# Fourier mixing and a gated FFN in one kernel: batch 0 turned on TensorE, DFT-47 of two batches inside the first tile

## The chip, the cores and the metric

The kernel runs on one core of a Trainium2 chip. The metric is the device time of one execution in microseconds; of the kernel before, three runs gave a median of 2671.09 us (2669.9 to 2671.72).

## The reference

`x` is 8 batches of 3008 positions by 256 channels, float32. The output is computed in two parts:

```
X  = rfft(x, axis=1)
Yr = Xr @ w_r - Xi @ w_i + b_r
Yi = Xr @ w_i + Xi @ w_r + b_i
Y  = soft threshold of Yr and Yi at 0.01
t  = irfft(Y, n=3008)            # 24064 tokens of 256
h  = t @ w_in                    # 256 x 2048
out = (h * sigmoid(1.702 h)) @ w_out
```

The weights of the second part come as float64 and are handed to the kernel as 64-bit words.

## The kernel before

**The Fourier part.** 3008 is 47 times 64, so the transform is done in two steps. Per batch: a DFT-47 (`stage_a`, constant `ka`) over 16 column blocks; a DFT-64 for 24 values of the 47 side, two per step `sp`, so 12 steps (`stage_b`, helper `dft64`, L278-286); the mixing with `w_r` and `w_i`, bias and threshold (`stage_mix`, `mixed` and `threshold`); and an inverse DFT-64 (`stage_inv`). The last inverse step, an inverse DFT-47, is done where tokens are fetched (`tokens`, constant `kz`). The DFT-47 contracts the position `n2` and the DFT-64 the position `n1`. Between the two the data change place between partitions and columns: `stage_a` writes its rows to a DRAM buffer `s1` (L308) and the next step reads them back in another view (L324, `rows`). All inverse results go to a DRAM buffer `s2`, from which `load_u` (L492) reads the columns for the tokens, all 96 rows at a time; so no token of a batch starts before that batch's last inverse step.

**Two forms of it.** `spectral_plain` (batches 0 and 1) works in float32 matrix products, of which the trace records two passes each. `spectral` (batches 2 to 7) splits each operand in a rounded high part and a rest and makes three products in the F32R type (`mm3`).

**The FFN.** Tokens come in 47 tiles of 512, and each tile takes 8 steps `q` over 256 of the 2048 hidden columns. `up(q)` makes 12 products of 512 columns, applies the activation on ScalarE (tile `gb`), and forms sums and high and low parts on ScalarE and VectorE (`hb`, `lb`, `gt`, `ht`, `lt`). `down` of the step before makes 21 products of 256 columns. Its 16 weight blocks (block 2q is `w_in` of step q, block 2q+1 `w_out`) are loaded by GpSimd's DMA queue and converted from float64 by ScalarE and VectorE (`from_float64`, `up_weights`, `down_weights`; tiles `aem` and `w`).

**The order of work.** The code is written in one order, and a scheduler with a model of time moves instructions forward on each engine where their inputs allow; each engine then runs its list in order. Before the first tile stand all of batch 0, the DFT-47 of batch 1 (`a1`) and weight blocks 0 to 7; the rest of batch 1 and blocks 8 to 15 are in a list `front`, taken during the first four FFN steps. The steps of batches 2 to 7 follow in a queue between FFN steps. Nothing holds the weight blocks in place, and the scheduler put all sixteen ahead of the first tile. The DMAs of loads, `s1`, `s2` and output all go through SP's queue, in its order.

Of the kernel before, what the change touches and what calls it, by code (L numbers as in the profile page):

```python
# [48 lines left out]
def constants():  # L49
# [59 lines left out]
    pack[:96, 524:618] = ai  # L109
    plain = np.zeros((128, 96), np.float32)  # L110
    plain[:96] = a
    return np.concatenate([plain, pack, packs], 1), b.astype(np.float32)


@with_exitstack
def fourier_mix_then_gated_ffn(ctx: ExitStack, tc: tile.TileContext, x, w_r, w_i, b_r, b_i, w_in, w_out, pack, kbs, out):
    nc = tc.nc
    NB = x.shape[0]
    NT = out.shape[0]
    a96, pack, packs = pack[:96, 0:96], pack[:, 96:96 + PK], pack[:, 96 + PK:96 + PK + PKR]  # L120
# [34 lines left out]
    def const(shape, dt, name):  # L155
        return cst.tile(shape, dt, name=name, tag=name.rstrip("_"))

    ka = const([96, 192], F32, "ka")
    ki = const([128, 512], F32, "ki")
    kz = const([96, 94], F32, "kz")  # L160
    fg = const([128, NS], F32, "fg")
# [128 lines left out]
                s2.rearrange("(s r) p j d -> s (r p j) d", r=2))  # L290


    def spectral_plain(b, s2):

        s1 = dr.tile([48, 2, NJ, D], F32, name="s1")
        s1w, s1r, s2w = dram_views(s1, s2)
        xs, ks, raw, rows, cos, mv = {}, {}, {}, {}, {}, {}

        def load_x(n):
            xs[n] = su.tile([96, 2, 512], F32, name="xp", tag="xp", bufs=6)  # L300
            nc.sync.dma_start(xs[n].rearrange("p a n -> p (a n)"), x[b, :, 1024 * n:1024 * (n + 1)])

        def stage_a(q):
            ps = bank()
            mm(ps[:96], ka[:, 0:96], xs[q // 2][:, q % 2])
            ev = buf2("aev")[:96]
            nc.scalar.copy(ev.rearrange("p j d -> p (j d)"), ps[:96])
            nc.sync.dma_start(s1w[:, 512 * q:512 * (q + 1)], ev.rearrange("p j d -> p (j d)"))  # L308

        def load_k(sp):  # L310
            ks[sp] = buf([128, 2, 2 * N1], F32, "kr") if b else su.tile([128, 2, 2 * N1], F32, name="k0", tag="k0", bufs=8)
            nc.sync.dma_start(ks[sp], kbs[sp])

        def load_b(sp):
            if sp not in ks:
                load_k(sp)
            k = ks[sp]
            if b:
                t = buf2("br")
                nc.sync.dma_start(t, s1r[2 * sp:2 * sp + 2].rearrange("s p d -> p s d"))  # L320
            else:
                if sp % 2 == 0:
                    rows[sp // 2] = su.tile([128, 4, D], F32, name="rows", tag="rows", bufs=6)
                    nc.sync.dma_start(rows[sp // 2], s1r[2 * sp:2 * sp + 4].rearrange("s p d -> p s d"))  # L324
                t = rows[sp // 2][:, 2 * (sp % 2):2 * (sp % 2) + 2]
            raw[sp] = t, k

        def stage_b(sp):
            for n in range(sp, sp + (2 if b else 3)):
                if n < 12 and n not in raw:  # L330
                    load_b(n)
            cos[sp] = dft64(*raw[sp])

        def stage_mix(sp):
            co = cos.pop(sp)
            pa, pb = bank(), bank()
            for v, ps in ((2, pa[:, 0:D]), (1, pb[:, 0:D]), (0, pb[:, D:])):
                for c in range(2):
                    mm(ps, co[:, c, v], wf[:, v, c], start=c == 0, stop=c == 1)
            v = mixed(pa, pb)  # L340
            threshold(v)
            mv[sp] = v

        def stage_inv(m):


            if b:
                po = [bank()[:, 0:D].rearrange("p (h d) -> p h d", h=1) for _ in range(2)]
            else:
                po = [ps_o.tile([128, 2, D], F32, name="pi", tag=f"po{2 * (m % 2) + i}") for i in range(2)]  # L350
            G = 1 if b else 2
            for h in range(G):
                sp = G * m + h
                v = mv.pop(sp)
                if sp:
                    kt = buf([128, 128], F32, "kt", bufs=1)
                    nc.scalar.mul(kt, kv[:, 1], fg[:, sp:sp + 1])
# [7 lines left out]
            if b:  # L365
                ev = buf2("iev")
                for i in range(2):
                    nc.scalar.copy(ev[:, i], po[i][:, 0])
                nc.sync.dma_start(s2w[2 * m:2 * m + 2].rearrange("s p d -> p s d"), ev)
                return  # L370
# [5 lines left out]
        return load_x, stage_a, load_k, load_b, stage_b, stage_mix, stage_inv  # L376


    def spectral(b, s2):
        s1 = dr.tile([48, 2, NJ, D], F32, name="s1")  # L380
        s1w, s1r, s2w = dram_views(s1, s2)
# [137 lines left out]
    class Ffn:  # L519
# [5 lines left out]
        def up(self, q):  # L525
            gb = fbuf([128, 4, HT], F32, "gb")
            for i in range(2):
                f = 2 * q + i
                ps = bank()
                fs = slice(128 * f, 128 * f + 128)  # L530
                for c in range(2):
                    mm3(ps, wi_h[:, c, fs], wi_l[:, c, fs], self.th[:, c], self.tl[:, c], start=c == 0, stop=c == 1)
                o = gb[:, 1:3] if i else gb[:, 0:4:3]
                nc.scalar.activation(o, ps.rearrange("p (h n) -> p h n", h=2), AF.Gelu_apprx_sigmoid)  # L534
# [11 lines left out]
            split(ht, lt, gt)  # L546
            self.g[q] = [(hb[:, i], lb[:, i]) for i in range(3)] + [(ht[:, i], lt[:, i]) for i in range(4)]

        def down(self, q):
# [36 lines left out]
            done += 1  # L586
        load_u(done)

    lx0, a0, lk0, lb0, b0, m0, i0 = spectral_plain(0, new_s2(0))
    lx1, a1, lk1, lb1, b1, m1, i1 = spectral_plain(1, new_s2(1))  # L590

    nc.sync.dma_start(ka[:, 0:96], a96)
    for n in range(6):
        lx0(n)
    load_weights(0)
    load_weights(1)
    mixer_in()
    for q in range(16):
        a0(q)
        if q in (1, 3):  # L600
            lx0(6 + q // 2)
        if q in (5, 7, 9):
            lx1((q - 5) // 2)
        if 5 <= q < 13:
            lk0(q - 5)
        if q in (6, 11):
            weights(q // 6 - (q > 6))
    for sp in range(0, 8, 2):
        lb0(sp)
    constants_in()  # L610
    for q in range(6):
        a1(q)
    for n in range(14):
        if n < 12:
            b0(n)
        if 1 <= n < 13:
            m0(n - 1)
        if n % 2 and n >= 3:
            i0((n - 3) // 2)
        if n % 2 == 0 and n < 12:  # L620
            weights(2 + n // 2)
        if 3 <= n < 8:
            lx1(n)
    for q in range(6, 16):
        a1(q)
    held.close()
    ff = ctx.enter_context(tc.tile_pool(name="ff", bufs=2, reuse_waits="tile"))

    front = []
    for n in range(14):  # L630
        if n < 12:
            front.append((b1, n))
        if 1 <= n < 13:
            front.append((m1, n - 1))
        if n >= 2:
            front.append((i1, n - 2))
        if n % 3 == 0 and n < 12:
            front.append((weights, 8 + 2 * n // 3))
            front.append((weights, 9 + 2 * n // 3))
    nf = len(front)  # L640

    tokens_to(TOK)
    queue, nextb, behind = [], 2, None
    for n in range(NT * NQ):
        k, q = divmod(n, NQ)
        if q == 0:
            cur = Ffn(k)
        cur.up(q)
        while front and len(front) * 4 > nf * (3 - n):
            step, m = front.pop(0)  # L650
            step(m)
        if not front and not queue and nextb < NB:
            if nextb == 2:
                rounded_parts()
# [52 lines left out]
```

## Time and profile before

| | |
|---|---|
| median of three runs | 2671.09 us |
| profiled execution | 2669.87 us |
| its span | 2668.1 us |
| TensorE busy | 2607.2 us (98%) |
| VectorE busy | 2001.8 us (75%) |
| ScalarE busy | 1563.2 us (59%) |
| mean granted TensorE clock | 0.988 |

The sums below are made against the profiled execution: 2669.87 us, of which 1.8 us lie outside its span. The matmul records are pipelined: the ends that the trace shows include the drain of the last one, so the pace of a stream is read from one start to the next.

### The profile page before, as it was taken

The numbers are of one execution on the slowest core, as the hardware profiler recorded it, in microseconds if no ns is written. First come the engines' busy times: TensorE is split into PE (matmuls) and PEld (weight loads), VectorE is DVE, ScalarE is ACT, GpSimd is POOL, SyncE is SP. The second block draws the span as 40 slices with busy tenths as digits, with TensorE's granted clock in tenths as the row PEclk, the third lists the DMA queues.
The fourth block names the chain that finished last, engine by engine and source line by source line (L and its number), as shares of the span: only waits on it lengthen the run. The fifth ranks groups of instructions, "written<-read, shape, count | busy, mean of one in ns | idle before, by whom it ended". The sixth has DMA issues, their size and how long they took to land. (4 is left out here: it accounts for less than half of the span.)

```text
span 2668.1 us, 42434 instructions
## 1 busy us (share of the span) xinstructions
PE 2607.2 (98%) x16562; PEld 2332.4 (87%) x16562; DVE 2001.8 (75%) x3287; ACT 1563.2 (59%) x2431; POOL 61.5 (2%) x69
## 2 busy tenths in 40 slices
PE   5889999999999999999999999999999999999998
PEld 2667899999989999899989999899998899999997
DVE  5945777777777777777877777778877787777776
ACT  3334655555575566656576555755567556655554
POOL 1000000000000000000000000000000000000000
PEclk7989999999999999999999999999999999999999
DMA  9343212121232223322232222422324122200000
GB/s 312 105 125 104 81 46 61 42 79 46 66 122 61 79 71 95 116 65 73 81 112 84 69 72 81 131 66 66 94 73 124 56 77 87 78 21 32 18 20 16
DMA packets 165176, 214.03 MB, mean 80 GB/s; under 512 B 16112, under 2 KB 115184, under 8 KB 164976
## 3 DMA queue, kind: packets, MB, share of 16 engines
q1 hardware_dynamic: 162512, 202.41, 25.2%
q0 software_dynamic: 2464, 8.91, 1.1%
q8 instruction: 130, 2.13, 0.3%
q14 instruction: 70, 0.57, 0.1%
HBM read 117.42 MB, written 93.85 MB: 79 GB/s over the span
## 5 line engine op out<-in xcount | busy, mean ns | idle before, releaser
L534 ACT ACTIVATE gb<-pa 128x512 f32<-128x512 f32 x752 | 448.1, 598 | 507.4 <-PE pa L145 505.3
L142 DVE TENSOR_TENSOR lt<-gt,ht 128x1024 fp32r<-128x1024 f32 x376 | 465.5, 1238 | 259.5 <-ACT ht L141 257.5
L145 PE MATMUL pa<-th,wi_h 128*128 128x512 f32 x1504 | 593.6, 395 | 0.5 <-ACT th L141 0.5
L145 PE MATMUL pa<-tl,wi_h 128*128 128x512 f32 x1504 | 592.1, 394 | 0.0
L145 PE MATMUL pa<-th,wi_l 128*128 128x512 f32 x1504 | 589.0, 392 | 0.0
L141 ACT CAST ht<-gt 128x1024 fp32r<-128x1024 f32 x376 | 394.1, 1048 | 254.2 <-DVE gt L545 253.7
L145 PE MATMUL po<-lt,wo_h 128*128 128x256 f32 x1504 | 411.1, 285 | 0.6 <-DVE lt L142 0.6
L145 PE MATMUL po<-ht,wo_l 128*128 128x256 f32 x1504 | 406.0, 283 | 0.0
L543 DVE TENSOR_TENSOR gt<-gb 128x512 f32<-128x512 f32 x376 | 259.2, 689 | 164.6 <-ACT gb L534 156.7
L142 DVE TENSOR_TENSOR lb<-gb,hb 128x768 fp32r<-128x768 f32 x376 | 362.0, 963 | 26.0 <-ACT hb L141 24.7
L145 PE MATMUL po<-ht,wo_h 128*128 128x256 f32 x1504 | 362.2, 284 | 1.6 <-ACT ht L141 1.4
L145 PEld LDWEIGHTS pa<-th,wi_l 128*128 128x128 f32 x1504 | 283.9, 189 | 55.5
L141 ACT CAST hb<-gb 128x768 fp32r<-128x768 f32 x376 | 314.4, 836 | 26.3 <-PE po L145 19.1
L145 PEld LDWEIGHTS pa<-th,wi_h 128*128 128x128 f32 x1504 | 284.8, 189 | 45.1 <-ACT th L141 0.7
L145 PEld LDWEIGHTS pa<-tl,wi_h 128*128 128x128 f32 x1504 | 285.0, 189 | 41.1
L145 PE MATMUL po<-lb,wo_h 128*128 128x256 f32 x1128 | 316.4, 284 | 1.8 <-DVE lb L142 1.8
L145 PE MATMUL po<-hb,wo_l 128*128 128x256 f32 x1128 | 315.7, 283 | 0.0
L145 PE MATMUL po<-hb,wo_h 128*128 128x256 f32 x1128 | 313.9, 291 | 0.0
L145 PEld LDWEIGHTS po<-lt,wo_h 128*128 128x128 f32 x1504 | 286.4, 190 | 9.2 <-DVE lt L142 0.8
L145 PEld LDWEIGHTS po<-ht,wo_l 128*128 128x128 f32 x1504 | 286.1, 191 | 5.7
L145 PEld LDWEIGHTS po<-ht,wo_h 128*128 128x128 f32 x1504 | 264.5, 190 | 12.0 <-ACT ht L141 1.6
L145 PEld LDWEIGHTS po<-hb,wo_h 128*128 128x128 f32 x1128 | 212.2, 190 | 12.4 <-issue 1.0
(93 smaller groups left out, 3531.5 us busy)
## 6 DMA issues: line engine op xcount, KB each, us to landing
s<-aev SPq DMA_DIRECT2D x128, 192.0 KB, 2.2
s<-iev SPq DMA_DIRECT2D x96, 256.0 KB, 2.2
ur<-s SPq DMA_DIRECT2D x128, 192.0 KB, 2.9
out<-o SPq DMA_DIRECT2D x94, 256.0 KB, 2.2
br<-s SPq DMA_DIRECT2D x84, 256.0 KB, 3.0
xr<-in_x SPq DMA_DIRECT2D x96, 192.0 KB, 3.0
yd<-mv SPq DMA_DIRECT2D x144, 128.0 KB, 2.4
yr<-yd SPq DMA_DIRECT2D x72, 256.0 KB, 3.0
```

Source lines behind the costliest of these rows:

```text
L141: nc.scalar.copy(hi, src)
L142: return nc.vector.tensor_tensor(lo, src, hi.bitcast(F32), ALU.subtract)
L145: nc.tensor.matmul(ps, lhsT=w, rhs=t, start=start, stop=stop)
L534: nc.scalar.activation(o, ps.rearrange("p (h n) -> p h n", h=2), AF.Gelu_apprx_sigmoid)
L543: nc.vector.tensor_tensor(gt[:, 0:2], b12, gb[:, 0:3:2], ALU.subtract)
```

## The change

Batch 0 gets a function of its own, `first_batch`. Its DFT-47 is written with the data as the stationary side: 64 products of 96 columns, whose results lie with channels on partitions. ScalarE copies them to an SBUF tile `z` (L310), and `turn` (L321) transposes 128x128 pieces of `z` on TensorE against an identity `one` into PSUM, from where ScalarE copies them to `rows` (L323). No DRAM buffer `s1` is used for batch 0. Only six of the sixteen DFT-47 blocks of batch 1 stay ahead of the first tile; its other ten and all sixteen of batch 2 (`dft47`, plain float32) are spread over the first seven FFN steps. The rest of batch 1 is done by `spectral`, in the split form, from the second tile on. `issue_after` ties hold weight blocks 0 to 7 behind named steps of batch 0 and blocks 8 to 15 behind the activation and the last split of the FFN steps of the first tile.

```diff
-    def spectral_plain(b, s2):
-
-        s1 = dr.tile([48, 2, NJ, D], F32, name="s1")
...
+    def first_batch(s2):
...
+        def stage_a(n):
+            t = xs.pop(n)
+            for c in range(2):
+                ps = bank()[:, 0:384].rearrange("p (j f) -> p j f", j=4)
+                for j in range(4):
+                    mm(ps[:, j], t[:, j, 128 * c:128 * c + 128], ka)
+                done_at["z", n] = nc.scalar.copy(z[:, c, :, 4 * n:4 * n + 4], ps.rearrange("p j f -> p f j")).ins
...
+        def turn(sp):
+            pt = ps_o.tile([128, 2, D], F32, name="pt", tag=f"po{2 + sp % 2}")
+            for i in range(2):
+                f = 4 * (2 * sp + i)
+                for c in range(2):
+                    nc.tensor.transpose(pt[:, i, 128 * c:128 * c + 128], z[:, c, f:f + 4].rearrange("p f j -> p (f j)"), one)
+            rows[sp] = su.tile([128, 2, D], F32, name="rows", tag="rows", bufs=4)
+            done_at["r", sp] = nc.scalar.copy(rows[sp], pt).ins
...
+    def dft47(b, q, t):
+
+        ps = bank()
+        mm(ps[:96], ka, t.rearrange("p j d -> p (j d)"))
+        ev = buf2("aev")[:96]
+        nc.scalar.copy(ev.rearrange("p j d -> p (j d)"), ps[:96])
+        s1w = s1s[b].rearrange("c p j d -> (c p) (j d)")
+        done_at["e"] = nc.sync.dma_start(s1w[:, 512 * q:512 * (q + 1)], ev.rearrange("p j d -> p (j d)")).ins
...
-        for n in range(16):
-            add(0, split_x, n, 16)
-            add(650, stage_a, n, 16)
-        steps.append((4000, lambda: None))
+        if not begun:
+            for n in range(16):
+                add(0, split_x, n, 16)
+                add(650, stage_a, n, 16)
+            steps.append((4000, lambda: None))
...
+    with after(("z", 7)):
+        weights(2)
...
+        if n % 2 == 0 and 2 <= n < 12:
+            with after(("v", n - 2), ("r", n)):
+                weights(2 + n // 2)
...
-    for q in range(6, 16):
-        a1(q)
+    for q in range(6):
+        dft47(1, q, x1[q // 2][:, 2 * (q % 2):2 * (q % 2) + 2])
...
+    early = [(1, q) for q in range(6, 16)] + [(2, q) for q in range(16)]
...
+        if n < NQ:
+            for m in range(8 + n + (n > 0), min(10 + n, 2 * NQ)):
+                with after("g", "l"):
+                    weights(m)
+            while nearly < len(early) * (n + 1) // 7 and nearly < len(early):
+                do_early(nearly)
+                nearly += 1
+        elif not queue and nextb < NB:
+            if nextb == 1:
+                with after("e"):
+                    rounded_parts()
             queue = spectral(nextb, new_s2(nextb))
```

Three places in the lists of instructions show what moves. The first is the start of TensorE's list; `pa<-xp,ka` is the DFT-47 of before, `pa<-ka,xp` that of the change, `pt` the transposes, `k` and `rows` the DFT-64, `wf` the mixing. Before:

```order
L145 MATMUL pa<-xp,ka 96x512 x22
L145 MATMUL pa<-k_144,rows 128x2x64 x4
L145 MATMUL pa<-k_151,rows 128x2x64 x4
L145 MATMUL pa<-wf,co 128x256 x6
L145 MATMUL pa<-k_178,rows 128x2x64 x4
```

Changed:

```order
L145 MATMUL pa<-ka,xp 128x96 x64
L321 MATMUL pt<-one,z 128x128 x8
L145 MATMUL pa<-k_179,rows 128x2x64 x4
L321 MATMUL pt<-one,z 128x128 x4
L145 MATMUL pa<-k_181,rows 128x2x64 x4
L321 MATMUL pt<-one,z 128x128 x8
L145 MATMUL pa<-wf,co 128x256 x6
L145 MATMUL pa<-k_183,rows 128x2x64 x4
L321 MATMUL pt<-one,z 128x128
```

Twenty-two DFT-47 blocks (16 of batch 0, 6 of batch 1) become 64 small products, and five steps' transposes stand ahead of the first mixing.

The second is VectorE's list where the first tokens (`tl`) come; `aem` and `w` are a weight block, `wo_l` its end, `mv` the threshold of a mixing step. Before, the last of the sixteen blocks ends right ahead of them:

```order
L269 SCALAR_TENSOR_TENSOR mv<-mv,mt 128x512
L253 TENSOR_TENSOR w_1501<-aem 128x2x128
L253 TENSOR_TENSOR w_1501<-aem 128x256
L256 TENSOR_TENSOR w_1501<-w_1501 128x128
L255 TENSOR_TENSOR w_1501<-w_1501 128x128
L257 TENSOR_TENSOR w_1501<-w_1501 128x128
L258 TENSOR_TENSOR w_1501<-w_1501 128x128
L142 TENSOR_TENSOR wo_l<-w_1501,wo_h 128x896
L142 TENSOR_TENSOR tl<-pa,th 128x2x188 x2
L142 TENSOR_TENSOR tl<-pa,th 128x2x136
L142 TENSOR_TENSOR tl<-pa,th 128x2x52
L285 TENSOR_TENSOR co<-co 128x2x128
L543 TENSOR_TENSOR gt<-gb 128x512
```

Changed, where `wo_l<-w_744` ends block 7:

```order
L142 TENSOR_TENSOR wo_l<-w_744,wo_h 128x896
L269 SCALAR_TENSOR_TENSOR mv<-mv,mt 128x512
L274 TENSOR_TENSOR mv<-pa,bias 128x512
L275 TENSOR_TENSOR mv<-pa,mv 128x512
L268 TENSOR_SCALAR mt<-mv 128x512
L269 SCALAR_TENSOR_TENSOR mv<-mv,mt 128x512
L142 TENSOR_TENSOR tl<-pa,th 128x2x188 x2
L142 TENSOR_TENSOR tl<-pa,th 128x2x136
L142 TENSOR_TENSOR tl<-pa,th 128x2x52
L556 TENSOR_TENSOR gt<-gb 128x512
L557 TENSOR_TENSOR gt<-gb,gt 128x256
L558 TENSOR_TENSOR gt<-gt,gb 128x256
L142 TENSOR_TENSOR lb<-gb,hb 128x768
L142 TENSOR_TENSOR lt<-gt,ht 128x1024
L231 TENSOR_SCALAR aem<-wraw 128x512 x2
L142 TENSOR_TENSOR tl<-pa,th 128x2x188
L232 SCALAR_TENSOR_TENSOR aem<-wraw,aem 128x512
```

Eight blocks stand ahead of the tokens where sixteen did, and blocks 8 and 9 begin behind the first step's `lt`.

The third is SP's queue between the last writes of batch 0 (`s_82<-iev`) and the reads for the first tokens (`ur`); `aev` are DFT-47 results on their way to `s1`. Before:

```order
L374 DMA s_82<-iev 128x2x256 x10
L184 DMA pk<-in_pack 128x822
L374 DMA s_82<-iev 128x2x256 x2
L308 DMA s_85<-aev 96x512 x9
L492 DMA ur<-s_82 96x512
L308 DMA s_85<-aev 96x512
L492 DMA ur<-s_82 96x512 x3
```

Changed:

```order
L359 DMA s_82<-iev 128x2x256 x8
L386 DMA s_86<-aev 96x512 x5
L655 DMA xr<-in_x 96x512 x2
L386 DMA s_86<-aev 96x512
L655 DMA xr<-in_x 96x512
L505 DMA ur<-s_82 96x512 x4
L655 DMA xr<-in_x 96x512 x2
```

Nine writes of DFT-47 results stood between the two; now six stand there, with three loads for the next DFT-47 blocks (`xr`).

## Rows read from the trace of the kernel before

**Rows 1.** The page's 40 slices: TensorE's granted clock in tenths.
```profile
PEclk7989999999999999999999999999999999999999
```

**Rows 2.** Windows: length; busy of PE, PEld, DVE, ACT, POOL; clock, DMA share, GB/s.
```profile
57.80:135.00 77.20, 67.74 (x344) 50.92 (x344) 72.45 (x152) 28.25 (x51) 5.93 (x8) 0.93 0.42 138
...
135.00:148.60 13.60, 7.23 (x14) 2.37 (x13) 1.70 (x4) 7.68 (x15) 0.00 (x0) 0.87 0.67 208
148.60:246.90 98.30, 90.93 (x508) 75.67 (x508) 52.26 (x90) 35.88 (x75) 0.00 (x0) 0.94 0.32 98
148.60:160.70 12.10, 10.79 (x43) 9.52 (x44) 2.23 (x5) 4.04 (x7) 0.00 (x0) 0.58 0.36 115
246.90:252.70 5.80, 5.68 (x13) 3.80 (x14) 3.48 (x6) 3.36 (x7) 0.00 (x0) 0.51 0.53 159
252.70:2658.30 2405.60, 2403.57 (x15631) 2189.22 (x15629) 1840.03 (x2971) 1465.31 (x2248) 47.30 (x46) 1.00 0.24 71
```

**Rows 3.** DMA, 0 to 60 us: totals; issues, KB each, us to landing.
```profile
DMA packets 9295, 18.38 MB, mean 306 GB/s; under 512 B 1369, under 2 KB 4490, under 8 KB 9293
...
xp<-in_x SPq DMA_DIRECT2D x16, 384.0 KB, 6.5
```

**Rows 4.** Timeline, PE, start-up: start, us, what, x records, [idle <-releaser].
```profile
5.95 7.51 PE L145 MATMUL pa<-xp,ka 96*96 96x512 f32 x12 [5.95 <-DMA xp<-in_x]
...
57.91 3.72 PE L145 MATMUL pa<-k,rows 128*128 128x128 f32 x16 [8.98 <-ACT aem L230]
```

**Rows 5.** Windows, instructions on tile aem (weight blocks) alone, on VectorE.
```profile
57.80:138.00 80.20, 36.44 (x68) 0.93 0.41 133
sum 138.00, DVE 59.47; mean DVE 29.74
```

**Rows 6.** The same for tile w (the down blocks' seven sums).
```profile
57.80:138.00 80.20, 15.55 (x37) 5.63 (x6) 0.93 0.41 133
sum 138.00, DVE 23.04 ACT 7.50; mean DVE 11.52 ACT 3.75
```

**Rows 7.** Timeline, PE, inside batch 0's loop.
```profile
82.23 1.05 PE L145 MATMUL pa<-k,rows 128*128 128x128 f32 x8
83.22 0.70 PE L145 MATMUL pi<-mv,ki 64*128 64x256 f32 x4
...
84.28 2.86 PE L145 MATMUL pa<-wf,co 128*128 128x256 f32 x12
86.98 1.05 PE L145 MATMUL pa<-k,rows 128*128 128x128 f32 x8
```

**Rows 8.** Timeline, PE, in the steady part; the last row is plain F32.
```profile
1004.10 0.85 PE L145 MATMUL pa<-yh,ki__1623 128*128 128x512 f32 x3
1004.79 0.28 PE L145 MATMUL po<-hb,wo_h 128*128 128x256 f32 x1
...
1010.96 0.28 PE L145 MATMUL pa<-wf_h,zz 128*128 128x256 f32 x1
...
1013.10 0.28 PE L145 MATMUL po<-hb,wo_h 128*128 128x256 f32 x1
...
122.98 1.10 PE L145 MATMUL pa<-xp,ka 96*96 96x512 f32 x2
```

**Rows 9.** Timeline, PE and SP, from batch 0's last inverse to the first tokens.
```profile
134.54 0.60 PE L145 MATMUL pi<-mv,kt 64*128 64x256 f32 x4
...
138.13 7.20 SPq L308 DMA_DIRECT2D s<-aev  x9
...
145.43 0.36 SPq L492 DMA_DIRECT2D ur<-s  x1
...
148.62 1.10 PE L145 MATMUL pa<-kz,ur 96*128 96x94 f32 x8 [3.37 <-DMA ur<-s]
```

**Rows 10.** Windows, instructions on tile gt alone (seventeen FFN steps), 300 to 400 us.
```profile
300.00:400.00 100.00, 46.71 (x67) 17.77 (x17) 1.00 0.17 52
```

**Rows 11.** The page's fifth part: VectorE's lb, whole run.
```profile
L142 DVE TENSOR_TENSOR lb<-gb,hb 128x768 fp32r<-128x768 f32 x376 | 362.0, 963 | 26.0 <-ACT hb L141 24.7
```

More of the change, by code (lines that the diff above doesn't have):

```diff
@@ L111, in constants @@
     plain[:96] = a
-    return np.concatenate([plain, pack, packs], 1), b.astype(np.float32)
+    return np.concatenate([plain, np.eye(128, dtype=np.float32), pack, packs], 1), b.astype(np.float32)
 @with_exitstack
@@ L290, in dram_views @@
                 s2.rearrange("(s r) p j d -> s (r p j) d", r=2))
-    def spectral_plain(b, s2):
-        s1 = dr.tile([48, 2, NJ, D], F32, name="s1")
-        s1w, s1r, s2w = dram_views(s1, s2)
-        xs, ks, raw, rows, cos, mv = {}, {}, {}, {}, {}, {}
-        def load_x(n):
[L300 to L308, printed above, removed]
+    def first_batch(s2):
+        s2w = s2.rearrange("(s r) p j d -> s (r p j) d", r=2)
+        xs, ks, rows, cos, mv = {}, {}, {}, {}, {}
+        z = su.tile([128, 2, 96, NJ], F32, name="z")
+        one = su.tile([128, 128], F32, name="one")
+        nc.gpsimd.dma_start(one, eye)
+        def load_x(n):
+            xs[n] = xpair(0, n)
+        def stage_a(n):
[5 more added lines that the diff above has]
+                done_at["z", n] = nc.scalar.copy(z[:, c, :, 4 * n:4 * n + 4], ps.rearrange("p j f -> p f j")).ins
@@ L310, in load_k @@
         def load_k(sp):
-            ks[sp] = buf([128, 2, 2 * N1], F32, "kr") if b else su.tile([128, 2, 2 * N1], F32, name="k0", tag="k0", bufs=8)
+            ks[sp] = su.tile([128, 2, 2 * N1], F32, name="k0", tag="k0", bufs=3)
             nc.sync.dma_start(ks[sp], kbs[sp])
[L314 to L326, printed above, removed]
+        def turn(sp):
[6 more added lines that the diff above has]
+            done_at["r", sp] = nc.scalar.copy(rows[sp], pt).ins
@@ L328, in stage_b @@
         def stage_b(sp):
[L329 to L332, printed above, removed]
+            cos[sp] = dft64(rows.pop(sp), ks.pop(sp))
         def stage_mix(sp):
@@ L340, in stage_mix @@
             v = mixed(pa, pb)
-            threshold(v)
+            done_at["v", sp] = threshold(v).ins
             mv[sp] = v
         def stage_inv(m):
[L347 to L353, printed above, removed]
+            po = [ps_o.tile([128, 2, D], F32, name="pi", tag=f"po{i}") for i in range(2)]
+            for h in range(2):
+                sp = 2 * m + h
                 v = mv.pop(sp)
@@ L374, in stage_inv, with xpair, after, new_s1 @@
                 nc.sync.dma_start(s2w[4 * m + i:4 * m + 4:2].rearrange("s p d -> p s d"), ev)
-        return load_x, stage_a, load_k, load_b, stage_b, stage_mix, stage_inv
+        return load_x, stage_a, load_k, turn, stage_b, stage_mix, stage_inv
+    def xpair(b, n):
+        t = su.tile([96, 4, D], F32, name="xp", tag="xp", bufs=5)
+        nc.sync.dma_start(t.rearrange("p j d -> p (j d)"), x[b, :, 1024 * n:1024 * (n + 1)])
+        return t
+    s1s, done_at = {}, {}
+    def after(*keys):
+        held = ExitStack()
+        for k in keys:
+            held.enter_context(tc.issue_after(done_at[k]))
+        return held
+    def new_s1(b):
+        s1s[b] = dr.tile([48, 2, NJ, D], F32, name="s1")
+    def dft47(b, q, t):
[5 more added lines that the diff above has]
+        done_at["e"] = nc.sync.dma_start(s1w[:, 512 * q:512 * (q + 1)], ev.rearrange("p j d -> p (j d)")).ins
     def spectral(b, s2):
-        s1 = dr.tile([48, 2, NJ, D], F32, name="s1")
-        s1w, s1r, s2w = dram_views(s1, s2)
+        begun = b in s1s
+        if not begun:
+            new_s1(b)
+        s1w, s1r, s2w = dram_views(s1s[b], s2)
         ka, ki, fg, wf_h, wf_l = (parts[n] for n in "aifhl")
@@ L545, in up @@
             nc.vector.tensor_tensor(gt[:, 3], gt[:, 2], gb[:, 1], ALU.subtract)
-            split(ht, lt, gt)
+            done_at["l"] = split(ht, lt, gt).ins
             self.g[q] = [(hb[:, i], lb[:, i]) for i in range(3)] + [(ht[:, i], lt[:, i]) for i in range(4)]
@@ L587, in tokens_to @@
         load_u(done)
[L589 to L593, printed above, removed]
+    lx0, a0, lk0, t0, b0, m0, i0 = first_batch(new_s2(0))
+    new_s1(1)
+    new_s1(2)
+    nc.sync.dma_start(ka, a96)
+    for n in range(5):
         lx0(n)
@@ L596, in fourier_mix_then_gated_ffn @@
     load_weights(1)
[L597 to L611, printed above, removed]
-        a1(q)
-    for n in range(14):
+    for n in range(8):
+        a0(n)
+        if n < 3:
+            lx0(n + 5)
+        if n == 3:
+            mixer_in()
+            constants_in()
+            for k in range(3):
+                lk0(k)
+        if n in (2, 4):
+            with after(("z", n)):
+                weights(n // 4)
+    with after(("z", 7)):
+        weights(2)
+    x1 = {}
+    for n in range(15):
+        if n == 0:
+            t0(0)
+        if n < 11:
+            t0(n + 1)
         if n < 12:
             b0(n)
+        if n < 9:
+            lk0(n + 3)
         if 1 <= n < 13:
@@ L619, in fourier_mix_then_gated_ffn, with load_early, do_early @@
             i0((n - 3) // 2)
[L620 to L623, printed above, removed]
-    for q in range(6, 16):
-        a1(q)
+        if n % 2 == 0 and 2 <= n < 12:
+            with after(("v", n - 2), ("r", n)):
+                weights(2 + n // 2)
+        if n in (4, 6, 8):
+            x1[n // 2 - 2] = xpair(1, n // 2 - 2)
+    for q in range(6):
+        dft47(1, q, x1[q // 2][:, 2 * (q % 2):2 * (q % 2) + 2])
     held.close()
     ff = ctx.enter_context(tc.tile_pool(name="ff", bufs=2, reuse_waits="tile"))
[L629 to L640, printed above, removed]
+    early = [(1, q) for q in range(6, 16)] + [(2, q) for q in range(16)]
+    xr = {}
+    def load_early(m):
+        if m < len(early):
+            b, q = early[m]
+            xr[m] = buf2("xr")[:96]
+            nc.sync.dma_start(xr[m].rearrange("p j d -> p (j d)"), x[b, :, 512 * q:512 * (q + 1)])
+    def do_early(m):
+        load_early(m + 3)
+        dft47(*early[m], xr.pop(m))
+    for m in range(3):
+        load_early(m)
+    nearly = 0
     tokens_to(TOK)
-    queue, nextb, behind = [], 2, None
+    queue, nextb, behind = [], 1, None
     for n in range(NT * NQ):
@@ L648, in fourier_mix_then_gated_ffn @@
         cur.up(q)
[L649 to L654, printed above, removed]
+        if n < NQ:
[9 more added lines that the diff above has]
+                    rounded_parts()
             queue = spectral(nextb, new_s2(nextb))
```

15 lines of the change are left out of this document (5 added, 10 removed).

## The prediction, made before the changed kernel ran

> **What bounds the kernel now.** I read the page's slices first, then windows, then the single streams. In the slices [rows 1] the clock is below full only in the first tenth of the run. The windows [rows 2] say the same of TensorE: from 252.7 us on it is busy 2403.57 of 2405.60 us at clock 1.00, so there nothing but TensorE's own work can change the time. All the slack lies ahead of that. So two questions set the forecast: when the first tokens start (148.62 us now, [rows 9]), and how much TensorE work and how many gaps lie behind them.
>
> The time to the tokens falls into three pieces. Up to 57.91 us, where the first DFT-64 starts [rows 4], the DMA is the limit: 18.38 MB in 60 us at 306 GB/s [rows 3]. From there to 135 us runs batch 0's loop; TensorE is busy 67.74 of 77.20 us, VectorE 72.45 [rows 2], so VectorE sets the pace, loaded with weight blocks that the first tile does not need. From 135 to 148.6 us batch 1's DFT-47 and the turn-round through `s2` follow [rows 9].
>
> **The change, part by part.**
>
> *To the first transpose.* Batch 0's trip through `s1` goes: 16 writes of 192 KB and as many bytes read, 6.3 MB. What must be in before the last DFT-47 product: 3.15 MB of `x`, three weight blocks (1.57), `w_r` and `w_i` (0.52), constants and the identity (0.7), five DFT-64 matrices (0.65): 6.6 MB, which at 306 GB/s [rows 3] takes 21.5 us. Counted from about 2 us that gives 23.5. But SP issues the sixth to eighth loads of `x` only as buffers come free, behind the constants, and such a load took 6.5 us to land [rows 3]; I add 2.5 us, then 3.7 us for the last eight products and their copy. The 64 products cost the pace of the tokens' products (eight records, four matmuls, in 1.10 us, [rows 9]), so 14 to 18 us in all, and hide behind the loads. First transpose at 29.5 us; 26 if the loads run at full rate, 35 if the last three loads wait for one another.
>
> *The loop.* A step costs TensorE 0.99 us for the DFT-64, 2.70 for the mixing, 1.06 for the inverse, from start to start in [rows 7]. New are four transposes. None is in this trace; the nearest row is the DFT-64 itself, four 128x128 products in 0.99 us. Below, half of it (if one pass does); above, twice (half clock). I take 0.99. Sum 5.74 us, twelve times 69. Four of the six DFT-47 blocks lie in the loop: about 1 us each, for a block's two records last 1.10 with the drain [rows 8]; 4 us. The stream begins at half clock, as it did at 57.91, where sixteen records took 3.72 us instead of twice 0.99 [rows 4, 7]: 4 us lost. VectorE no longer sets the pace: of the sixteen blocks, 52 us fell into its loop (36.44 on `aem`, 15.55 on `w`, [rows 5, 6]) out of 82.5 in all, 5.2 each. Now six blocks lie there, 31 us, so its load falls from 72 to about 52 us, below TensorE's 69. I leave 2 us of waits. The loop takes 79 us and ends at 108.5.
>
> *The transposes and the clock.* In this trace real matmuls at 95% busy keep the clock at 0.93 to 1.00 [rows 2], and no row shows a transpose. The Trainium skill, page "TensorE: Matmul & The Clock Gate", section "Part 4: PE-mode transpose", says that the full clock does not engage for transposes, since they do not count as TensorE work in the same way; it speaks against this change. Under that rule the sum would have the 48 transposes at half clock, 12 us more. I stay with the row, because each group of four stands between matmuls.
>
> *To the tokens.* Now 13.5 us pass from the last inverse (its end about 135.1) to the tokens, because `ur` was issued at 145.43, behind nine `aev` writes that held SP for 7.20 us [rows 9]. Six writes and three loads stand there now, and most of the DFT-47 results are ready earlier. From `ur`'s issue to the products 3.2 us pass [rows 9]; I put 5.8 us ahead of that for the two copies, the last writes and SP's line, 9 in all (bounds 6.6 and 13.5). Tokens start at 117.5 instead of 148.6: 31.1 us earlier.
>
> *TensorE's work behind the tokens.* Batch 1's mixing and inverse change form: plain 2.70 + 1.06 = 3.76 us a step [rows 7], split 2.14 + 0.69 = 2.83 [rows 8], so 11.2 us less. Ten DFT-47 blocks move from before to behind: 8.6 to 11 us more. Batch 2's sixteen go from three split products (0.69, [rows 8]) to plain ones (at least 0.86): 2.7 us more. The sum is 0.1 us, up to 4: taken as 0.
>
> *Gaps behind the tokens.* Before: 5.1 us to the half clock (12.1 us at 0.58), 2.8 more (5.8 us at 0.51), and 7.4 idle out of 98.3 [rows 2]; 15.3 us. Now the cold start stays. In the first tile VectorE has eight blocks (41 us at most) and eight FFN steps at 46.71/17 + 0.96 = 3.71 us [rows 10, 11], 30 us: with the tokens' parts 73. TensorE has eight times 5.3 (12 products at 0.23, 21 at 0.12, [rows 8]), 26 DFT-47 blocks (22) and the tokens (3): 67. So VectorE leads by a little, and TensorE loses about 6 us. Then ScalarE must wait for the mixing weights that batch 1's split form needs, as it had to for batch 2's inside the 7.4 us above; I put 5 us there. Sum 16 us, 1 more.
>
> *Sum.* 2669.87 - 31.1 + 0 + 1 = 2639.8 us. The profiled execution was 1.2 us under the median of its runs; on that scale 2641. I say **2640 us**.
>
> **The rivals.**
>
> *The first tile gives part of it back* (0.2). Blocks 8 to 15 were hidden by idle TensorE before; now they stand on VectorE in order between `lt` of one step and `gt` of the next, and `down` waits for `lt`. For it: VectorE's 73 us against 67. Against: a block is due only when its own step comes, some steps later. If half of the 41 us shows, the time is 2640 + 20 - 6 = 2654. If all of it shows, 2674: no change (0.04).
>
> *Faster than forecast* (0.12): loads at full rate (-3.5), transposes in one pass (-6), `ur` without a queue (-2.4), no lag of VectorE (-6): 2622.
>
> *The clock stays low in the loop* (0.04). This ends on the other side. If transposes drag the granted clock of the whole loop down to half, its 73 us of TensorE work become 146: tokens at 29.5 + 148 + 9 = 186, 38 us later than now, 2709. It decides from a mean granted clock of 0.66 in the loop, where 73 us become the 110 that would bring the tokens to 148.6. Against it: transposes are a sixth of the loop's work. [...]
>
> *The change does not do what it says* (in the 0.04 of no change): the blocks would have to be moved ahead of the loop again. The changed list has eight of them there, so only waits could bring that about.
>
> **How the numbers follow.** The forecast has 0.6. A measurement of this kernel tells about 0.2%, 5 us, from no change. Faster by more: 0.6 + 0.2 + 0.12 = 0.92; within: 0.04; slower: 0.04. For the range: the start-up reaches from -3.5 to +5.5, transposes from -6 to +12, the tail from -2.4 to +4.5, the first tile from -6 to +14. They are independent; combined by their squares about -10 and +20, and I let the lower end reach most of the faster case: 2624 to 2660.
>
> **What would show it.** Right: first transpose near 29.5 us, loop of about 79 us with TensorE ahead of VectorE in busy time, tokens near 117.5, first tile with VectorE above 90% and TensorE gaps of some 6 us, later stretches as now. Wrong: a granted clock near 0.5 where `pt` products run; TensorE waiting for `z` copies or `xp` beyond 35 us; `ur` issued more than 10 us behind the last inverse; gaps above 15 us in the first tile that end with `lt`, `hb` or `wf_h`; or TensorE work behind the tokens that grew by more than 4 us.

## The result, and the profile after

| | before | changed |
|---|---|---|
| median | 2670.49 us of 4 runs (2668.55 to 2671.72) | 2629.45 us of 4 runs (2627.32 to 2632.74) |
| profiled execution | 2669.87 us | 2629.47 us |
| its span | 2668.1 us | 2627.7 us |
| TensorE busy | 2607.2 us | 2598.6 us |
| mean granted clock | 0.988 | 0.994 |

The changed kernel takes 0.9848 of the time before, interval 0.9831 to 0.9865: 41 us less, and 10.5 us less than the 2640 us forecast. The start of TensorE's timeline answers to [rows 4]. Its columns are start, length, line and operation, then how many records, and in brackets the idle time ahead and what ended it:

```profile
5.50 17.35 PE L145 MATMUL pa<-ka,xp 96*128 96x96 f32 x80 [5.50 <-DMA xp<-in_x]
24.23 10.53 PE L145 MATMUL pa<-ka,xp 96*128 96x96 f32 x48 [1.38 <-DMA xp<-in_x]
34.55 2.32 PE L321 MATMUL pt<-one,z 128*128 128x128 f32 x8
36.91 1.69 PE L145 MATMUL pa<-k,rows 128*128 128x128 f32 x8
38.44 0.60 PE L321 MATMUL pt<-one,z 128*128 128x128 f32 x4
38.87 1.06 PE L145 MATMUL pa<-k,rows 128*128 128x128 f32 x8
39.77 1.04 PE L321 MATMUL pt<-one,z 128*128 128x128 f32 x8
40.64 2.76 PE L145 MATMUL pa<-wf,co 128*128 128x256 f32 x12
43.23 1.05 PE L145 MATMUL pa<-k,rows 128*128 128x128 f32 x8
```

The DFT-64 starts at 36.91 us, where it was 57.91. The DFT-47 fills TensorE from 5.50 to 34.55 with one wait of 1.38 us: it is TensorE that sets this piece, not the loads (e6 tests that). Four transposes take 0.43 us from their start (38.44) to the next (38.87): one record each. The DFT-64 step behind them takes 0.90 us from start to start and the mixing step (`wf`) 2.59, no more than the 0.99 and 2.70 of [rows 7].

Windows of the changed kernel answer to [rows 2]. The columns are again length; busy time of TensorE, weight loads, VectorE, ScalarE and GpSimd; clock, DMA share and GB/s:

```profile
34.50:106.70 72.20, 71.36 (x394) 53.66 (x393) 57.85 (x115) 30.11 (x58) 4.35 (x6) 1.00 0.32 103
106.70:118.00 11.30, 2.39 (x5) 0.57 (x4) 0.00 (x0) 4.08 (x8) 0.00 (x0) 0.63 0.83 257
118.00:130.40 12.40, 11.87 (x38) 9.51 (x39) 1.81 (x4) 4.04 (x7) 0.00 (x0) 0.51 0.20 63
118.00:190.00 72.00, 70.99 (x326) 51.36 (x327) 55.82 (x106) 47.10 (x77) 3.57 (x5) 0.92 0.58 179
190.00:210.00 20.00, 18.07 (x110) 15.86 (x109) 17.94 (x34) 13.30 (x24) 0.00 (x0) 1.00 0.39 119
118.00:2617.90 2499.90, 2494.97 (x16169) 2263.79 (x16169) 1937.72 (x3162) 1528.75 (x2352) 49.48 (x51) 1.00 0.26 78
```

In batch 0's loop (first row) TensorE is busy 99% and VectorE 80%. The clock column reads 1.00 there; that it was full from about 38 us on is told by the pace of the DFT-64 and mixing above, since the column is not to be trusted so early (last section). In the kernel before, TensorE was busy 67.74 of 77.20 us there and VectorE 72.45 [rows 2]. In the first tile (fourth row) TensorE idles 1.0 us in 72, with VectorE at 78%. That is a mean over two parts: up to 130.4 us (third row) VectorE has only 1.81 us of work, and in the 59.6 us from there on it is busy 54.0, which is 91%. Behind the tokens (last row) TensorE idles 4.9 us in all.

The turn-round to the tokens answers to [rows 9]; `SPq` is SP's queue, and the last row is TensorE's:

```profile
108.31 3.01 SPq L386 DMA_DIRECT2D s<-aev  x5
111.91 0.79 SPq L655 DMA_DIRECT2D xr<-in_x  x2
...
113.69 3.15 SPq L505 DMA_DIRECT2D ur<-s  x4
```

```profile
118.05 5.41 PE L145 MATMUL pa<-kz,ur 96*128 96x94 f32 x24 [7.33 <-DMA ur<-s]
```

Tokens start at 118.05 us instead of 148.62: 30.6 us of the 40.4 us between the two spans. The other 9.8 us come from behind the tokens: the stretch from there to the end of the span fell from 2519.5 to 2509.7 us.

### The profile page after: what moved, and what is told of

It is laid out like the page before. It is cut to its first block, busy times and chain, and to the rows that moved or that the text cites. A ratio compares the mean times of both kernels' runs of the same rounds, so it can differ in the third digit from the quotient of the medians.

```text
span 2627.7 us, 42749 instructions
## 1 busy us (share of the span) xinstructions
PE 2598.6 (99%) x16705; PEld 2347.1 (89%) x16705; DVE 2011.5 (77%) x3307; ACT 1575.4 (60%) x2440; POOL 60.4 (2%) x70
```

## The experiments

All runs compare with the changed kernel's median, 2629.45 us. The runs of the kernel before beside each group had medians of 2670.7 to 2671.7 us. The changed kernel's own four runs span 5.4 us, so a difference of 2 us (e5, e6) is not told from none by the times alone; there the traces carry the argument. The first four take one part of the change back or double it.

### e1: the ties on blocks 8 to 15 taken off

```diff
-                with after("g", "l"):
-                    weights(m)
+                weights(m)
```

> The tie on weight blocks 8 to 15 is taken away, all else stays; in VectorE's list six of them now end ahead of the first tokens. If the tie gives a real part of the gain (theory), VectorE again sets the pace of batch 0's loop: 57.9 us of work there become about 85, above TensorE's 72, and the tokens come 8 to 15 us later than at 118.0; the first tile gives nothing back since TensorE is full there; about 2638 us. If the tie is only order (rival), the blocks find room beside TensorE and the time stays within 3 us of 2629.

Measured: 2636.63 us (2635.11 to 2637.68), ratio to before 0.9875 (0.9858 to 0.9891), 7.2 us more than the change. The blocks went back ahead of the first tile. Windows of this kernel for the loop and the stretch from there to the tokens, then two rows of TensorE's timeline:

```profile
34.80:113.00 78.20, 72.14 (x394) 54.23 (x393) 70.86 (x145) 35.30 (x67) 5.78 (x8) 0.96 0.34 108
113.00:128.10 15.10, 3.73 (x4) 0.98 (x5) 11.42 (x24) 6.83 (x12) 1.64 (x3) 0.50 0.87 269
```

```profile
108.82 1.23 PE L145 MATMUL pi<-mv,ki 64*128 64x256 f32 x4 [2.45 <-DVE mv L269]
...
114.45 3.73 PE L145 MATMUL pa<-xp,ka 96*96 96x512 f32 x4 [3.55 <-ACT aev L384]
```

VectorE is busy 70.86 us in the loop where the change has 57.85, and TensorE falls to 92%. But TensorE keeps step with the change until about 100 us (its last mixing starts at 95.29, in the change at 95.08). Only then does it wait: for thresholds from VectorE (`mv`, 2.5 us and 0.7), so that the loop's last product ends at 110.9 instead of 106.7, and then for ScalarE's copies of DFT-47 results (`aev`, 3.55 us). The tokens come at 128.11 us, 10 later. In the profiled execution 4.5 us of that come back behind them, by the medians 2.9. So blocks that the first tile did not need yet delay the last steps of the loop and the turn-round; that they pace the whole loop is not shown here.

### e2: batch 2's DFT-47 not in the first tile

```diff
-    new_s1(2)
...
-    early = [(1, q) for q in range(6, 16)] + [(2, q) for q in range(16)]
+    early = [(1, q) for q in range(6, 16)]
```

> Only batch 1's ten DFT-47 blocks stay in the first tile; batch 2's sixteen go back to the split form in their own turn. If they are filler for a first tile in which VectorE would else set the pace (theory), TensorE gets 13.7 us less to do there and waits instead, while the same work comes back later: 5 to 12 us slower, about 2637 us, with idle time of TensorE in the first tile. If only the count of TensorE's work matters (rival), it is 2.7 us faster, 2627 us.

Measured: 2643.32 us (2641.11 to 2644.46), ratio 0.9897 (0.9883 to 0.9912): 13.9 us more. The window of the first tile, then the chief waits of TensorE from 119 to 400 us behind the tokens' own (us in total, times, longest):

```profile
119.00:190.00 71.00, 58.64 (x280) 46.46 (x281) 55.97 (x107) 39.55 (x63) 3.57 (x5) 0.84 0.38 115
```

```profile
PE pa L145 <- ACT wi_h L242: 6.6, 2, 3.7
PE po L145 <- DVE lt L142: 3.2, 2, 2.5
PE po L145 <- ACT ht L141: 2.1, 2, 1.1
```

Without the sixteen blocks TensorE idles 12.4 us of 71 and waits for weight blocks (`wi_h`) and for the split of the activations (`lt`, `ht`). The mean clock there falls from 0.92 to 0.84. So the tied weight blocks do make TensorE wait, and batch 2's DFT-47 is the work that covers it. Of the parts taken back this is the largest, and more than was expected of it.

### e3: batch 0 through DRAM again

```diff
-                for j in range(4):
-                    mm(ps[:, j], t[:, j, 128 * c:128 * c + 128], ka)
...
+                mm(ps[:96], ka, t[:, 2 * c:2 * c + 2].rearrange("p j d -> p (j d)"))
...
+                nc.sync.dma_start(s1w[:, 512 * q:512 * (q + 1)], ev.rearrange("p j d -> p (j d)"))
...
-                    nc.tensor.transpose(pt[:, i, 128 * c:128 * c + 128], z[:, c, f:f + 4].rearrange("p f j -> p (f j)"), one)
...
+            done_at["r", sp] = nc.sync.dma_start(rows[sp], s1r[2 * sp:2 * sp + 2].rearrange("s p d -> p s d")).ins
```

> Batch 0 goes through its DRAM buffer again: DFT-47 in 512-column products, 16 writes, 12 reads; no transposes. All else as changed. If most of the earlier start comes from what was moved away from the start (batch 1's loads and blocks, weight blocks 8 to 15), the first DFT-64 comes at 42 to 48 us instead of 36.9, the loop is 5 us shorter without transposes, and the whole is 2 to 8 us slower, about 2634 us. If the DRAM trip itself held the start until 57.9 us (rival), the first DFT-64 stays near 55 us and the time is about 2643 us.

Measured: 2635.17 us (2634.45 to 2635.51), ratio 0.9868 (0.9853 to 0.9882): 5.7 us more. TensorE's timeline of this kernel in the DFT-47, around the first DFT-64, and at the tokens:

```profile
6.19 8.12 PE L145 MATMUL pa<-xp,ka 96*96 96x512 f32 x12 [6.19 <-DMA xp<-in_x]
14.53 1.93 PE L145 MATMUL pa<-xp,ka 96*96 96x512 f32 x4 [0.22 <-DMA xp<-in_x]
...
30.90 3.70 PE L145 MATMUL pa<-xp,ka 96*96 96x512 f32 x4 [0.43 <-DMA xp<-in_x]
44.31 3.75 PE L145 MATMUL pa<-k,rows 128*128 128x128 f32 x16 [9.71 <-DMA rows<-s]
...
121.66 3.70 PE L145 MATMUL pa<-kz,ur 96*128 96x94 f32 x16 [8.45 <-DMA ur<-s]
```

The DRAM trip makes TensorE wait 9.71 us, and the DFT-64 starts 7.4 us later than in the change (44.31 against 36.91), but 13.6 earlier than in the kernel before. So most of the 21 us at the start came from what no longer stands there, batch 1's loads and DFT-47 blocks and the weight blocks; the ties on blocks 8 to 15 are not in it, since without them (e1) the first transpose still starts at 34.85 us, and the others were not taken apart. The turn on TensorE, together with the form of DFT-47 that it needs, is worth 5.7 us of the 41.

### e4: every transpose done twice

```diff
-                    nc.tensor.transpose(...)
+                    for _ in range(2):
+                        nc.tensor.transpose(...)
```

> Every transpose is made twice, 48 more. The trace shows four in 0.44 us. If the transposes lie on the path of the loop (theory): 48 times 0.109, 5 us slower, 2634.5 us, and no drop of the granted clock in the loop. If they hide beside other work: no change. If transposes pull the clock down (the rule weighed in the prediction), more than 10 us slower with a granted clock below 0.9 in the loop.

Measured: 2636.22 us (2635.66 to 2637.07), ratio 0.9872 (0.9857 to 0.9887): 6.8 us more. The loop's window, and the transposes (tile `pt`) alone in it:

```profile
36.00:113.00 77.00, 76.19 (x441) 58.53 (x439) 59.51 (x115) 30.83 (x59) 4.28 (x6) 1.00 0.30 95
```

```profile
36.00:113.00 77.00, 15.53 (x96) 12.10 (x95) 7.02 (x12) 1.00 0.30 95
```

With 96 transposes the DFT-64 and mixing keep their pace (0.90 and 2.60 us from start to start), and the clock column reads 1.00. The loop is 4.8 us longer than in the change; 1.3 us more lie ahead of the first transpose, in a longer wait for a load, and have nothing to do with the doubling. So the twelve groups cost some 5 us and do not slow the rest.

### e5, e6, e7: warm products at the start, and the loads first

TensorE needed 0.217 us for a product of 96 columns in the first 23 us (17.35 over 80 records), which over 128 records makes 27.8 us. The next runs ask how much of this can be had. First (e5), twelve products of a zero tile stand ahead of the DFT-47; their result is not used.

```diff
...
+    wp = bank()
+    for _ in range(12):
+        mm(wp[:, 0:128], wt, wt)
```

> Twelve 128-column products on a tile of zeros are added ahead of batch 0's DFT-47, while TensorE waits for the first load. DFT-47 in the changed form ran at 0.214 us a record from 5.5 to 34.5 us, the pace that the tokens' products of the same shape have at a granted clock of 0.51; the early clock column reads 1.00 there. If the clock was at 1.2 GHz all that time for want of a start (theory A), the products bring it up by about 10 us, the DFT-47 then waits for loads and ends about 27 us: 5 to 7 us faster. If the form of these products itself keeps the clock down (theory B), the pace stays at 0.21 and the time within 2 us of 2629. If the pace comes from the weight loads and not the clock (theory C), also no change, and the records of the added products show it: 0.11 us each where the clock is full.

Measured: 2631.5 us (2630.88 to 2631.68), 2.1 us more than the change, where 5 to 7 less were expected: a miss. TensorE's timeline, then two windows:

```profile
5.87 5.55 PE L145 MATMUL pa<-ka,xp 96*128 96x96 f32 x48
12.59 2.00 PE L145 MATMUL pa<-ka,xp 96*128 96x96 f32 x16 [1.17 <-DMA xp<-in_x]
15.64 3.70 PE L145 MATMUL pa<-ka,xp 96*128 96x96 f32 x16 [1.05 <-DMA xp<-in_x]
25.12 10.52 PE L145 MATMUL pa<-ka,xp 96*128 96x96 f32 x48 [5.78 <-DMA xp<-in_x]
```

```profile
15.00:16.00 1.00, 0.36 (x2) 0.39 (x3) 0.66 (x2) 0.10 (x1) 0.00 (x0) 0.79 1.02 385
16.00:38.00 22.00, 16.04 (x73) 15.03 (x73) 11.26 (x23) 7.50 (x15) 1.42 (x2) 0.50 0.92 228
```

The pace does come up (48 records in 5.55 us), but then TensorE runs out of `x`: it waits twice, the clock falls to 0.50 at about 16 us, and the last 48 records run at half pace again behind a wait of 5.78 us.

Second (e6), all eight loads of `x` are issued before anything else. The last three have halves of their own to land in, so that no buffer has to come free.

```diff
+                xs[n] = [buf2("xh2")[:96] for _ in range(2)]
...
-    for n in range(5):
+    for n in range(8):
         lx0(n)
...
-        if n < 3:
-            lx0(n + 5)
```

> All eight loads of batch 0 go out first, the last three in halves into other buffers; constants and DFT-64 matrices follow. If DFT-47 is held by TensorE's pace (theory), only the 1.4 us wait at 24.2 us goes: 1 to 2 us faster. If it is held by the loads, as the prediction had it (rival), it ends at about 24 us: 8 us faster or more.

Measured: 2627.63 us (2627.32 to 2627.74), 1.8 us less than the change: the 1.38 us wait is gone, the first transpose starts at 32.55 us, 2.0 earlier, and the DFT-47 still runs at half pace, without a wait. So the loads did not hold it. Then both edits together (e7):

> Both: the added products and the loads first. Theory A: DFT-47 ends at about 22 us, tokens 12 us earlier, 2617 us. Theory B: as e6, 2628 us.

Measured: 2624.47 us (2622.29 to 2626.06), ratio 0.9827 (0.9812 to 0.9841), 5.0 us less than the change and less than half of what was expected. The first transpose starts at 27.83, but short waits for loads were left and the clock was at half again from about 20 to 33 us:

```profile
18.49 2.98 PE L145 MATMUL pa<-ka,xh 96*128 96x96 f32 x16 [0.93 <-DMA xh<-in_x]
21.75 6.29 PE L145 MATMUL pa<-ka,xh 96*128 96x96 f32 x28 [0.28 <-DMA xh<-in_x]
27.83 2.32 PE L327 MATMUL pt<-one,z 128*128 128x128 f32 x8
```

### e8: the six early DFT-47 blocks of batch 1 moved behind as well

```diff
-    for q in range(6):
-        dft47(1, q, x1[q // 2][:, 2 * (q % 2):2 * (q % 2) + 2])
...
-    early = [(1, q) for q in range(6, 16)] + [(2, q) for q in range(16)]
+    early = [(b, q) for b in (1, 2) for q in range(16)]
```

> The six DFT-47 blocks of batch 1 that stood ahead of the tokens go into the first tile with the others. Tokens come earlier: the four blocks inside the loop took 4 us, and the reads for the tokens no longer stand behind six writes and three loads on SP, 4 us more; about 110 us instead of 118. Behind them TensorE has six blocks more, 5.1 us. Theory (both hold): 2 to 3 us faster, 2627 us. If the reads' latency and not SP's line sets the wait: 1 us slower.

Measured: 2634.15 us (2632.27 to 2637.58), ratio 0.9868 (0.9851 to 0.9884), 4.7 us more: a miss. The tokens come at 109.38 us, 8.7 earlier, but the first tile pays for it. TensorE's waits from 109 to 230 us:

```profile
PE pa L145 <- DMA ur<-s: 6.9, 1, 6.9
PE pa L145 <- DMA xr<-in_x: 5.8, 6, 2.2
```

Six waits for `xr` (5.8 us), which the change does not have, and the moved work itself lies behind the tokens, some 5 us by an estimate from the 0.86 us that a block takes in the change's first tile. Six blocks ahead of the tokens were better than none; no number between was tried.

### f1, f3, f4, f5: products that fill the waits

Here TensorE is kept at work through waits by products whose results are not used. First (f1) 5 products in the last inverse step and 24 ahead of the tokens:

```diff
...
+        if (b, q) == (1, 5):
+            wp = ps_o.tile([128, 2, D], F32, name="wp", tag="po2")
+            for _ in range(24):
+                mm(wp[:, 0, 0:128], wt[:96], ev[:, 0, 0:128])
```

> Only products whose results are not used are added, 5 behind the last inverse and 24 behind the last DFT-47 block ahead of the tokens, where TensorE waits 7.3 us for the reads. In the changed kernel the granted clock fell to 0.50 at about 110 us and came back at 130.4 us; in that stretch 12.4 us were run at 0.51, so 6 us are lost. If the clock stays up over the wait (theory), the first tile's start runs at full clock: 4 to 6 us faster, 2624.5 us. If it falls all the same (rival), the added products take 10 us at half clock and the tokens come 3 to 5 us later: 2633 us.

Measured: 2632.96 us (2631.27 to 2633.47), 3.5 us more than the change, a difference near the edge of what the scatter lets tell. TensorE's timeline:

```profile
114.54 8.18 PE L145 MATMUL wp<-aev,wt 96*128 96x128 f32 x48 [0.67 <-ACT aev L388]
122.56 2.81 PE L145 MATMUL pa<-kz,ur 96*128 96x94 f32 x24
```

The tokens' 24 records now run at full clock, 2.81 us instead of 5.41. But the clock had fallen before the fill began, so the fill ran slow, took 8.18 us and started the tokens 4.5 us later. Windows ahead of the fill and over its first part:

```profile
110.00:114.00 4.00, 2.27 (x4) 0.57 (x4) 0.00 (x0) 3.58 (x8) 0.00 (x0) 0.89 0.63 202
114.00:118.00 4.00, 3.46 (x16) 3.46 (x17) 0.00 (x0) 0.49 (x1) 0.00 (x0) 0.50 0.92 276
```

The clock's mean is 0.89 in the first window, already below full, and 0.50 in the second, in which the fill begins (114.54).

Second (f3), both this and the start: warm products, `x` first, and four products behind each of the DFT-47 steps 2 to 6, where e7 had waited; and third (f4), the start's part alone.

```diff
...
+        if n in (2, 3, 4, 5, 6):
+            with after(("z", n)):
+                spin(4, "po0")
```

> All of it: products on a tile of zeros ahead of batch 0's DFT-47 and between its steps, its loads first, and the products ahead of the tokens. With the clock up from the start (theory), DFT-47 ends at about 24 us instead of 27.8 in the run with warm products and early loads, transposes and the first DFT-64 run at full clock, 2 to 3 us more, and the tokens' start gives 5: 2614 us. If filling does not hold the clock over the waits for loads, no better than that run, 2624 us.

> As the run with everything, without the added products at the tokens: warm products, loads first, products between the steps of DFT-47. If the start alone carries that run's 9 us (theory), 2620 to 2622 us; if the products ahead of the tokens carried half of it (rival), 2625 us.

Measured: with both, 2620.31 us (2616.83 to 2622.9); with the start's part alone, 2620.63 us (2620.37 to 2620.76), ratio 0.981 (0.9797 to 0.9824). That is 8.8 us less than the change, so the start carries it and the fill at the tokens adds nothing that can be told. In the trace with both the fill did run at full pace (48 records in 5.62 us), but the tokens started at 112.02 us, 2.2 later than without it. TensorE's timeline of the start's part alone, and a window of it:

```profile
24.36 2.37 PE L145 MATMUL pa<-ka,xh 96*128 96x96 f32 x20
26.57 1.08 PE L145 MATMUL wp<-wt 128*128 128x128 f32 x8
27.49 1.04 PE L327 MATMUL pt<-one,z 128*128 128x128 f32 x8
...
109.86 5.40 PE L145 MATMUL pa<-kz,ur 96*128 96x94 f32 x24 [8.04 <-DMA ur<-s]
```

```profile
5.00:27.00 22.00, 19.65 (x169) 18.95 (x168) 10.96 (x22) 9.49 (x19) 1.20 (x2) 1.00 1.00 263
```

The first transpose starts 7.1 us earlier than in the change, and eight take 1.04 us where they took 2.32. Tokens come 8.2 us earlier, and 8.8 us are won. Records of 96 columns keep a pace of 0.11 us to the end of the DFT-47 (20 of them from 24.36 to 26.57), so TensorE stays at full clock through the start, idle 2.35 of 22 us. f4 is 51 us under the kernel before beside it; no other version measured is clearly faster.

Last (f5), f3 with more fill at the tokens:

```diff
-            for _ in range(24):
+            for _ in range(33):
                 mm(wp[:, 0, 0:128], wt[:96], ev[:, 0, 0:128])
```

> As the run with everything, with 33 instead of 24 products ahead of the tokens. There 24 took 5.6 us and left 2.0 us without work, and the first tile then ran at half clock until about 121 us. If the gap is what lets the clock fall (theory), closing it keeps the clock at full and saves 3 us: 2617 us. If the clock falls before (rival), the products run at half clock and the tokens are 2 to 4 us later: 2624 us.

Measured: 2623.79 us, scattered from 2616.82 to 2628.06. In its profiled execution (2625.5 us) the fill (66 records) took 10.09 us, and tokens started at 117.95. Here, as in f1, the clock had fallen before the fill began (0.50 from 107 to 108 us, the fill from 108.03), in f3 it had not. Whether that changes from run to run is open, since of each kernel only one execution has a trace.

## Why the prediction was right, and where its terms were wrong

The sign, the place and the mechanism held: tokens 31.1 us earlier were forecast, 30.6 measured. But that this number came out so close is luck: three errors cancel in it, and the rest of the gain lies in the term that was set to about nothing.

| piece | forecast | measured |
|---|---|---|
| first transpose | 29.5 us | 34.55 us |
| loop | 79 us | 72.2 us |
| loop's end to tokens | 9 us | 11.3 us |
| tokens at | 117.5 us | 118.05 us |
| behind the tokens | 1 us more | 9.8 us less |

**To the first transpose: 5 us late.** The step that failed is "14 to 18 us in all, and hide behind the loads". The 128 records took 27.7 us (17.35, and 10.32 from 24.23 to 34.55), since the pace was 0.217 us a record where the forecast took the tokens' 1.10 us for eight records, 0.14 each with the drain. The changed kernel's tokens, 5.41 us for 24 records at a clock of 0.51, show the pace that fits. The prediction itself put the first DFT-64 at half clock, and the DFT-47 right ahead of it at full. Moving the loads first gave only 1.8 us; loads first with a warm TensorE and its waits filled gave 8.8. The bound was TensorE at half clock, with the loads close behind it: in e5 a faster TensorE only waited longer for them. A cold start alone does not explain the half clock. In the old form (e3) the pace rose by itself at the same place: twelve records of 512 columns took 8.12 us, the next four 1.93. In the new form it never rose, in e6 not even over 128 records without a wait, though warmed ahead they ran fast (e5). So the new form seems to be part of the cost. No run tests that by itself, and e3 has a later stretch, eight records in 7.52 us behind a wait of 3.21, in which the old form did not rise either.

**The loop: 7 us early.** Priced between "half of it" and "twice", the transposes came out a little under the lower bound: 0.43 us per four against 0.99 taken, 6.7 us over twelve groups. Doubling them made the loop 4.8 us longer. The rest of the loop came out right only in sum: its first sixteen records lost about 2 us to half clock where 4 were put, TensorE waited 0.8 us instead of 2, and some 3 us of TensorE's work beyond the forecast, a remainder that no run explains, stand against that. TensorE stood ahead of VectorE in busy time, as forecast, though VectorE had 57.85 us of work and not 52. The rival that the clock stays low in the loop did not come, by the pace of DFT-64 and mixing, with 48 transposes and with 96. The reading that matmuls at 95% busy keep the clock up was too simple all the same: [rows 2] has a window with 5.68 us of 5.80 busy at a clock of 0.51. The Trainium skill, page "TensorE: Matmul & The Clock Gate", section "Part 4: PE-mode transpose", says that the full clock does not engage for transposes; for transposes among matmuls this trace does not agree (eight took 2.32 us in the half-clock start and 1.04 at 39.77 us, drain included), and no run here has them alone for long.

**To the tokens: 2 us late.** Five `aev` writes held SP for 3.01 us and three `xr` loads stood there; `ur` was issued 7.0 us behind the loop's end (113.69 against 106.7), where 5.8 were put, and 4.4 us passed to the products instead of 3.2.

**Behind the tokens: the mis-sized term.** "Sum 16 us" of gaps was forecast, against 15.3 before. Measured are 4.9 us of idle time and, at a clock of 0.51 over 12.4 us, 6.1 us lost to half clock: 11 in all. Before, the windows of [rows 2] give 9.5 idle and 7.9 lost to the clock, 17.4. That is 6.4 us of the 9.8. The other 3.4 are what is left for TensorE's own work, priced at 0.1; no run separates its three items, so this part stays open. The step that failed inside is "VectorE leads by a little": eight blocks and eight FFN steps were summed to 73 us from single durations. VectorE was busy 55.82 of 72 us and then 17.94 of 20, and TensorE barely waited for it. That it would be above 90% held, but only from 130.4 us on. Its instructions overlap, as the starts in its timeline show:

```profile
136.68 0.42 DVE L231 TENSOR_SCALAR aem<-wraw 128x512 int32<-128x512 int32 x1
137.01 0.54 DVE L142 TENSOR_TENSOR tl<-pa,th 128x376 fp32r<-128x376 f32 x1
137.47 0.68 DVE L232 SCALAR_TENSOR_TENSOR aem<-wraw,aem 128x512 int32<-128x512 int32 x1
138.07 0.68 DVE L556 TENSOR_TENSOR gt<-gb 128x512 f32<-128x512 f32 x1
```

Each begins some 0.08 us before the one ahead ends, which over a block of eight to fourteen instructions is about 1 us of 5. From 118 to 190 us VectorE did seven blocks and seven steps, whose single durations sum to some 64 us where it was busy 55.82. And the 5 us set aside for ScalarE ahead of batch 1's mixing did not appear: TensorE's waits from 190 to 212 us are 2.0 us in all, for the split parts `tl` and `zz`.

So the "first tile gives part of it back" rival did not come, but only because batch 2's DFT-47 stood there: without it (e2) the time rose by 13.9 us, with waits for `lt`, which the rival named, and for `ht` and the weight blocks' `wi_h`, the longest, which it did not. Of the 41 us, taking back one part alone costs 13.9 (batch 2's filler), 7.2 (ties on blocks 8 to 15) and 5.7 (the turn). These need not add up, and they leave 14 us of the 41; the ties on the first blocks and batch 1's ten blocks were not taken back alone.

## What to carry to other kernels

Work that the start does not need belongs where the bound engine already waits, and it needs its partner: late weight blocks make waits, and independent products of a later batch fill them (13.9 us here). Price an instruction at the clock that it will run at; in the first stage and behind the wait for the first tokens that was half, and work thought to be hidden behind loads became the bound. Where loads set the pace, having them all issued first pays only together with an engine that is fast enough to take them (1.8 us alone, nothing from the warm products alone, 5.0 together, 8.8 with the waits filled). A price taken from a warm stream does not hold for a stage that may never warm up (0.217 us a record here against 0.116).

## What was not expected of the hardware

The clock column is not to be relied on ahead of its first change. In the changed kernel this window reads 1.00, while 80 records take 17.35 us:

```profile
5.50:23.00 17.50, 17.35 (x80) 17.11 (x80) 7.40 (x13) 5.50 (x12) 0.00 (x0) 1.00 1.05 286
```

The same records take 0.116 us in e5 after warm products, and 0.219 there once its column shows 0.50 (10.52 us for 48). So in the first 38 us the pace of records tells the clock, and the column does not; in the changed kernel it first leaves 1.00 at about 110 us.

A 128x128 float32 transpose is one record of 0.11 us at full clock, where a float32 product of 128 columns is two. Steady work does not always bring the clock up: in e6 128 records of 96 columns stayed at half pace for 27 us without a wait, where 512-column products in e3 rose within their first dozen. And a clock once gained was soon lost: in e5 TensorE waited 1.17 and 1.05 us for loads, and from 16 us on the level was 0.50.
